# Inverse of cumulative decay products in a gated linear attention with a feed-forward layer: VectorE's reciprocal instead of ScalarE's logarithm and exponential with a Newton step

## The chip, the cores and the metric

The kernel runs on one core of one Trainium2 chip. The metric is the time of one execution on the device in microseconds (us); of several runs the median is given.

## What is computed

The reference is a gated linear recurrence for 4 batches of 8 heads, 768 tokens and a head dimension of 48, followed by a dense layer of two matrices on the 3072 tokens of width 384:

```
for t in range(S):
    state = alpha[:, :, t, :, None] * state + einsum('bhd,bhe->bhde', k[:, :, t], v[:, :, t])
    y[:, :, t] = einsum('bhd,bhde->bhe', q[:, :, t], state)
h  = x @ w_in                      # x is y, 3072 x 384; w_in is 384 x 2048
sp = maximum(h, 0) + log1p(exp(-abs(h)))
out = (h * erf(sp)) @ w_out        # w_out is 2048 x 384
```

All values of alpha lie between 0.8 and 1.

## The kernel before

**Chunks.** The recurrence is worked off in 24 chunks of 128 tokens, six for each batch, and all heads of a batch at once: a tile of 128 x 4 x 128 holds eight heads as four pairs, two heads above each other in the partitions, with the tokens along the free dimension. Inside a chunk, A is the running product of alpha. Queries are multiplied by A and keys by its inverse w, so that a masked product of the two gives all decays within the chunk; a state T carries what came before. The steps of a chunk are methods:

- ld loads alpha, k, q and v by SyncE's queue, and a ScalarE instruction (L141) notes values of alpha that are too large.
- a1 makes A by four scans of VectorE, one for each pair (L146; the trace calls the operation TENSOR_TENSOR_SCAN, the lists of instructions SCALAR_TENSOR_TENSOR), and GpSimd copies its last column (L151).
- a2 makes the inverse. ScalarE takes Ln of A (L155) into r, a tile in PSUM, and Exp of minus that (L156), which also sums r into flags. VectorE then makes a Newton step from r: A times r (L158), and (A r - 2) r (L159). The result w is minus the inverse.
- a3 makes K = k w (L164) and Q = q A (L166) on VectorE.
- a4 multiplies K and Q on TensorE for all pairs (pS, L174), masks the products on VectorE (sT, L180) with a mask of -1 and 0, which takes the minus sign out, and turns K for the state (pn, L187, and kn, L189).
- a5 multiplies with v and the state (py, L199 and L205), copies the result to y (L209), and brings the state T forward (L214, L224 for the first chunk of a batch, L228 and L229 for the others); the minus sign of K is undone there by a subtraction or by a factor of -1.
- a6 turns y into the block's x on TensorE (px, L254) and writes it as a high part (x_hi, ScalarE, L256) and a low part (x_lo, VectorE, L257).

**Blocks.** The dense layer works on 12 blocks of 256 tokens, two chunks each. H multiplies x by w_in (ph, L272, three matmuls for each pair of tiles for the high and low parts), and ScalarE reads it twice (w by Exp, L283, and hs, L284). L1 takes three functions of it on ScalarE (L289 to L291), L2 a Newton step on VectorE (t, L297, and w, L298). E switches ScalarE's table, applies Gelu (s, L303) and switches back. Z combines on VectorE (s, L308, and hs, L309). O splits the result into a high part gh (L320 on VectorE or L322 on ScalarE) and a low part gl (VectorE, L323), and multiplies both by w_out (acc, L331). The result goes out at L339.

**Weights.** They come as pairs of 32-bit words of a 64-bit number. Each of 28 pieces is put together by one ScalarE and three VectorE instructions (L360 to L368) and split into two parts (L343 on ScalarE, L344 on VectorE). All this lies in the first part of the run, among the steps of the first chunks.

**Order.** Three lists give the order of the steps: START (the weights, chunks 0 to 6 and the first blocks), ORDER (once for each block in between, with two chunks) and TAIL (the end). The framework's scheduler then lays out the instructions of each engine, and may put an instruction ahead of one that the lists give out earlier. Each engine works its own instructions in that order. Tiles of PSUM that the chunks use, r among them, come from one pool of four buffers (ps_at).

ScalarE's functions belong to tables. The helper tab ties the instructions that need the Ln and Exp table, L155 and L156 too, to the stretch between two table loads.

Of the kernel before, what the change touches and what calls it, by code (L numbers as in the profile page):

```python
# [10 lines left out]
F32 = mybir.dt.float32  # L11
# [4 lines left out]
AF = mybir.ActivationFunctionType  # L16
ALU = mybir.AluOpType
# [6 lines left out]
SAT = 4.0  # L24
RT2 = 2.0**0.5
LNEXP, GELU = "natural_log_exp_and_others", "gelu_and_others"
# The order in which the steps of chunks (128 tokens) and blocks (256) are given out: the start with the weights, the
# same for each block in between, and the end.
START, ORDER, TAIL = (
    z.split()  # L30
    for z in (
# [18 lines left out]
def gla_moe(ctx: ExitStack, tc: tile.TileContext, q, k, v, alpha, w_in, w_out, out):  # L50
    nc = tc.nc
    B, CPB, _, D, NP, P = q.shape
# [11 lines left out]
    const = ctx.enter_context(tc.tile_pool(name="const", bufs=1))  # L64
    fast = ctx.enter_context(ExitStack())
    raw = fast.enter_context(tc.tile_pool(name="raw", bufs=1))
    at = fast.enter_context(tc.tile_pool(name="at", bufs=2))
# [11 lines left out]
    for nm, fill in (("a", 1.0), ("q", 0.0), ("k", 0.0)):  # L79
# [3 lines left out]

    ident = const.tile([P, P], F32, name="ident")
    make_identity(nc, ident)
    maskn = const.tile([P, P], F32, name="maskn")
    nc.gpsimd.memset(maskn, -1.0)
    nc.gpsimd.affine_select(
        out=maskn, in_=maskn, pattern=[[1, P]], compare_op=ALU.is_ge, fill=0.0, base=0, channel_multiplier=-1
    )  # L90
    fixed = const.tile([P, 5], F32, name="fixed")
    floor, bhi, bsat, bone, ones = (fixed[:, n : n + 1] for n in range(5))
# [22 lines left out]
    def tab(ins):  # L115
        for p in phase["prev"]:
            tc.add_manual_dep(ins.ins, p.ins.name, NOSYNC, reason="tables")
        phase["cur"].append(ins)
        return ins
# [4 lines left out]
    class Chunk:  # L124
# [26 lines left out]
            nc.gpsimd.tensor_copy(out=self.ae, in_=self.A[:, :, P - 1])  # L151

        def a2(self):
            r = ps_at.tile([P, NP, P], F32, name="r", tag="at")
            tab(nc.scalar.activation(r, self.A, AF.Ln))  # L155
            tab(nc.scalar.activation(r, r, AF.Exp, scale=-1.0, accum_out=flags[:, self.n, 0:1]))  # L156
            w = at.tile([P, NP, P], F32, name="w", tag="w", bufs=1)
            nc.vector.tensor_tensor(out=w, in0=self.A, in1=r, op=ALU.mult)  # L158
            nc.vector.scalar_tensor_tensor(out=w, in0=w, scalar=2.0, in1=r, op0=ALU.subtract, op1=ALU.mult)  # L159
            self.w = w  # L160

        def a3(self):
# [5 lines left out]
        def a4(self):  # L168
            self.sT = []
            pss = [ps_at.tile([P, NP, P], F32, name="pS", tag="at") for _ in range(2)]  # L170
            for pair in range(NP):
                for par in range(2):
                    rows = slice(par * HD, par * HD + D)
                    nc.tensor.matmul(  # L174
                        out=pss[par][:, pair, :], lhsT=self.K[rows, pair, :], rhs=self.Q[rows, pair, :],
                        start=True, stop=True,
                    )
            for ps in pss:
                st = at.tile([P, NP, P], F32, name="sT", tag="sT")
                nc.vector.tensor_tensor(  # L180
                    out=st, in0=ps, in1=maskn.unsqueeze(1).broadcast_to([P, NP, P]), op=ALU.mult
                )
                self.sT.append(st)
            if not self.last:
                pn = ps_at.tile([P, NP, P], F32, name="pn", tag="at")
                for pair in range(NP):
                    nc.tensor.transpose(pn[:, pair, :], self.K[:, pair, :], ident)  # L187
                self.kn = at.tile([P, NP, 2, HD], F32, name="kn", tag="kn", bufs=1)
                nc.scalar.activation(  # L189
                    self.kn.rearrange("p a b d -> p (a b d)"), pn.rearrange("p a t -> p (a t)"), AF.Copy  # L190
                )

        def a5(self):
# [16 lines left out]
            if not self.last:  # L210
                pu = ps_at.tile([P, 512], F32, name="pu", tag="at")
                for pair in range(NP):
                    for par in range(2):
                        nc.tensor.matmul(  # L214
                            out=pu[par * HD : (par + 1) * HD, pair * D : (pair + 1) * D],
                            lhsT=self.kn[:, pair, par, :], rhs=vt[:, 2 * pair + par, :], start=True, stop=True,
                        )
                U = pu[:, : NP * D].rearrange("p (a d) -> p a d", a=NP)
                aeb = self.ae.unsqueeze(2).broadcast_to([P, NP, D])
                for par in range(2):  # L220
                    rows = slice(par * HD, (par + 1) * HD)
                    Tp, Up, ap = T[rows, :, par, :], U[rows], aeb[rows]
                    if self.first:
                        nc.vector.scalar_tensor_tensor(  # L224
                            out=Tp, in0=Up, scalar=-1.0, in1=ap, op0=ALU.mult, op1=ALU.mult
                        )
                    else:
                        nc.vector.tensor_tensor(out=Tp, in0=Tp, in1=Up, op=ALU.subtract)  # L228
                        nc.vector.tensor_tensor(out=Tp, in0=Tp, in1=ap, op=ALU.mult)  # L229

        def a6(self, moe):
# [6 lines left out]
    class Moe:  # L238
# [7 lines left out]
            self.x = (x_hi, x_lo)  # L246

        def turn(self, y, c, pool, tag):
            """Writes the 128 tokens of y, transposed, to the block's x as two parts."""
            x_hi, x_lo = self.x  # L250
            cs = slice(c * P, (c + 1) * P)
            px = pool.tile([P, 512], F32, name="px", tag=tag)
            for kt in range(KT):
                nc.tensor.transpose(px[:, kt * P : (kt + 1) * P], y[:, kt * P : (kt + 1) * P], ident)  # L254
            pxv = px[:, : KT * P].rearrange("p (a t) -> p a t", a=KT)
            nc.scalar.activation(x_hi[:, :, cs], pxv, AF.Copy)  # L256
            nc.vector.tensor_tensor(out=x_lo[:, :, cs], in0=pxv, in1=x_hi[:, :, cs].bitcast(F32), op=ALU.subtract)  # L257
# [86 lines left out]
        nc.vector.tensor_tensor(out=lo, in0=src, in1=hi.bitcast(F32), op=ALU.subtract)  # L344

    def weight(hi, lo, src, n, pool, tag):
        """Loads a matrix of float32, or of float64 as pairs of int32, and splits it into two parts."""
        if src.dtype == F32:
            t = pool.tile([P, n], F32, name="wst", tag=tag)
            nc.sync.dma_start(out=t, in_=src)  # L350
# [1 line left out]
            return  # L352
        st = pool.tile([P, n, 2], I32, name="wst", tag=tag)
        nc.sync.dma_start(out=st.rearrange("p n two -> p (n two)"), in_=src.bitcast(I32))
        # The scale takes 112 from the exponent that a high word has as a float32: its 5 low bits are left, and
        # what float32 has no exponent for goes to zero. Shifted by 3, the word ends where a float32's would.
        low, high = st[:, :, 0], st[:, :, 1].bitcast(F32)
        buf = keep_w.tile([P, 1024], F32, name="wbuf", tag="w")
        y, z = buf[:, :n], buf[:, 512 : 512 + n].bitcast(I32)
# [19 lines left out]
        weight(wo_hi[:, f, :], wo_lo[:, f, :], w_out[f * P : (f + 1) * P, :], DM, keep_s, "s")  # L379

    def general():
        """Any inputs: the recurrence token by token, then the same layers."""
        with ExitStack() as es:
            dram = es.enter_context(tc.tile_pool(name="g_dram", bufs=1, space=bass.MemoryType.DRAM))
            NG4 = P // (B * H)
# [69 lines left out]
    moes = [Moe(i * TB, pools) for i in range(NBLK)]  # L455

    def run(order, c0, b0):
        """The steps of a list: a chunk's count from c0, a block's (after @) from b0; past the end there are none."""
        for step in order:
            name, _, rel = step.partition("@")  # L460
            name, *arg = name.split("_")
# [20 lines left out]
        run(ORDER, 2 * i + 3, i)  # L482
    run(TAIL, 2 * NBLK, NBLK - 1)

    # lanes with a sum of inverse products, a gain, or an exponential past what the way above can carry
    top = const.tile([P, 3], F32, name="top")
    nc.vector.tensor_reduce(
        out=top[:, 0:2], in_=flags.rearrange("p n two -> p two n"), op=ALU.max, axis=mybir.AxisListType.X
# [54 lines left out]
```

## Time and profile before

| | us |
|---|---|
| median of 2 runs | 597.95 |
| the 2 runs | 597.25 and 598.65 |
| span of the profiled execution, first to last instruction | 594.3 |
| busy, PE (TensorE) | 552.4 |
| busy, DVE (VectorE) | 503.0 |
| busy, ACT (ScalarE) | 485.1 |

The profiled execution has a span and no time of its own on the page; the runs' median stands 3.65 us above that span. In rows of the profile a group is a line of the kernel, an engine, an operation and its tiles, with the count, then the busy time in us and the mean of one in ns, and then the engine's idle time just before them with what ended it. Rows in order of time begin with the start in us and the duration in us. Matmuls overlap, so their durations add up to more than PE's busy time.

### The profile page before, as it was taken

The page shows a single profiled execution, that of the slowest core. Times are in us where ns is not written, and L with a number is a line of the kernel's source. Part 1 is how long each engine was busy: PE and PEld are TensorE (multiplying, and loading weights), DVE is VectorE, ACT ScalarE, POOL GpSimd, SP SyncE. Part 2 cuts the span into 40 slices and gives each one's busy share as a digit, 9 for nine tenths or more (in the row PEclk, how much of TensorE's full clock was granted, in tenths as well). Part 3 has the DMA queues.
Part 4 walks back from the last instruction along what each step waited for, and adds up shares of the span by engine and source line. Part 5 has one row for each costly group of instructions (what it writes and reads, how often), then busy time and mean ns, then how long its engine had stood idle before and what let it go on. Part 6 is the DMA issues. An engine that isn't in the chain of part 4 may idle for free.

```text
span 594.3 us, 11033 instructions
## 1 busy us (share of the span) xinstructions
PE 552.4 (93%) x4282; PEld 534.8 (90%) x4282; DVE 503.0 (85%) x769; ACT 485.1 (82%) x845; POOL 20.9 (4%) x40
## 2 busy tenths in 40 slices
PE   0679798999999999999999999999999999999994
PEld 0568787999999999999999999999999999999884
DVE  7899999999999869869779879879779879758780
ACT  4558979698989879889879879889788888889941
POOL 1000110002000000000000000000000000000000
PEclk9999798998999999999999999999999999999998
DMA  6584312313112102112112102112112101000001
GB/s 196 176 290 145 110 55 81 120 54 94 28 41 81 41 26 68 41 29 68 40 28 68 41 28 67 41 39 70 28 35 66 34 28 41 1 1 28 1 27 33
DMA packets 20220, 36.98 MB, mean 62 GB/s; under 512 B 3520, under 2 KB 9664, under 8 KB 20160
## 3 DMA queue, kind: packets, MB, share of 16 engines
q1 hardware_dynamic: 20160, 36.19, 19.9%
q8 instruction: 36, 0.59, 0.4%
q14 instruction: 24, 0.20, 0.1%
HBM read 31.46 MB, written 4.72 MB: 61 GB/s over the span
## 4 chain that ended last, share of the span: by engine, by line
PE 81%; DVE 9%; ACT 6%; DMA 2%; issue 1%; SPq 0%; ACTq 0%; DVEq 0%
PE acc L331 33%; PE ph L272 30%; PE py L205 7%; PE pS L174 4%; PE py L199 3%; PE pu L214 2%; DMA wst<-in_moe_w_in_dram 2%; PE pn L187 1%; PE px L254 1%; DVE hs L309 1%; DVE s L308 1%; DVE A L146 1%; ACT wbuf L360 1%; ACT w L283 1%; DVE wbuf L365 1%
## 5 line engine op out<-in xcount | busy, mean ns | idle before, releaser
L272 PE MATMUL ph<-x_hi,wi_hi 128*128 128x256 f32 x576 | 164.0, 288 | 4.0 <-ACT hs L284 3.4
L272 PE MATMUL ph<-x_lo,wi_hi 128*128 128x256 f32 x576 | 163.4, 284 | 0.4 <-DVE x_lo L257 0.4
L272 PE MATMUL ph<-x_hi,wi_lo 128*128 128x256 f32 x576 | 163.2, 284 | 0.0
L331 PE MATMUL acc<-wo_hi,gh 128*128 128x384 f32 x384 | 134.5, 351 | 3.6 <-DVE gh L320 2.6
L331 PE MATMUL acc<-wo_lo,gh 128*128 128x384 f32 x384 | 131.3, 342 | 0.0
L331 PE MATMUL acc<-wo_hi,gl 128*128 128x384 f32 x384 | 130.0, 344 | 1.2 <-DVE gl L323 1.2
L272 PEld LDWEIGHTS ph<-x_hi,wi_hi 128*128 128x128 f32 x576 | 110.4, 192 | 5.8 <-ACT hs L284 4.2
L272 PEld LDWEIGHTS ph<-x_lo,wi_hi 128*128 128x128 f32 x576 | 110.5, 192 | 0.7 <-DVE x_lo L257 0.7
L272 PEld LDWEIGHTS ph<-x_hi,wi_lo 128*128 128x128 f32 x576 | 110.5, 192 | 0.5 <-DVE wi_lo L344 0.5
L283 ACT ACTIVATE w<-ph 128x512 f32<-128x512 f32 x96 | 57.5, 599 | 46.9 <-PE ph L272 44.0
L297 DVE TENSOR_TENSOR t<-s,w 128x1024 f32<-128x1024 f32 x48 | 58.5, 1219 | 29.4 <-ACT w L291 29.3
L331 PEld LDWEIGHTS acc<-wo_hi,gh 128*128 128x128 f32 x384 | 72.8, 190 | 5.3 <-DVE gh L320 2.6
L331 PEld LDWEIGHTS acc<-wo_hi,gl 128*128 128x128 f32 x384 | 72.2, 190 | 2.6 <-DVE gl L323 2.6
L323 DVE TENSOR_TENSOR gl<-hs,gh 128x512 fp32r<-128x512 f32 x96 | 65.3, 683 | 10.8 <-ACT gh L322 10.3
L331 PEld LDWEIGHTS acc<-wo_lo,gh 128*128 128x128 f32 x384 | 73.2, 191 | 0.0
L205 PE MATMUL py<-raw_v,sT 128*128 128x48 f32 x384 | 57.9, 279 | 5.5 <-DVE sT L180 5.5
L308 DVE TENSOR_TENSOR s<-s,w 128x1024 f32<-128x1024 f32 x48 | 58.2, 1218 | 2.3 <-ACT s L303 2.1
L205 PEld LDWEIGHTS py<-raw_v,sT 128*128 128x128 f32 x384 | 53.8, 203 | 6.8 <-DVE sT L180 6.6
L298 DVE SCALAR_TENSOR_TENSOR w<-t,w 128x1024 f32<-128x1024 f32 x48 | 58.4, 1217 | 0.4
L309 DVE SCALAR_TENSOR_TENSOR hs<-s,hs 128x1024 f32<-128x1024 f32 x48 | 58.2, 1217 | 0.3
L289 ACT ACTIVATE s<-w,fixed 128x1024 f32<-128x1024 f32 x48 | 55.1, 1151 | 0.0
L284 ACT ACTIVATE hs<-ph 128x512 f32<-128x512 f32 x96 | 54.8, 593 | 0.0
(67 smaller groups left out, 834.2 us busy)
## 6 DMA issues: line engine op xcount, KB each, us to landing
wst<-in_moe_w_in_dram SPq DMA_DIRECT2D x12, 512.0 KB, 4.6
wst<-in_moe_w_out_dram SPq DMA_DIRECT2D x16, 384.0 KB, 3.4
raw_a<-in_alpha_dram SPq DMA_DIRECT2D x48, 96.0 KB, 2.2
raw_k<-in_k_dram SPq DMA_DIRECT2D x48, 96.0 KB, 2.2
raw_q<-in_q_dram SPq DMA_DIRECT2D x48, 96.0 KB, 2.2
raw_v<-in_v_dram SPq DMA_DIRECT2D x24, 192.0 KB, 2.4
out_dram<-o SPq DMA_DIRECT2D x24, 192.0 KB, 1.9
```

The source lines that it names most:

```text
L174: nc.tensor.matmul(out=pss[par][:, pair, :], lhsT=self.K[rows, pair, :], rhs=self.Q[rows, pair, :], start=True, stop=True,)
L205: nc.tensor.matmul(out=py[:, h * D : (h + 1) * D], lhsT=self.sT[par][:, pair, :], rhs=vt[:, h, :], start=self.first, stop=self.first or pa ...
L272: nc.tensor.matmul(out=o, lhsT=wt[:, kt, fs], rhs=xt[:, kt, :], start=n == 0, stop=n == 3 * KT - 1)
L283: tab(nc.scalar.activation(w, ph, AF.Exp, accum_out=self.pl.flags[:, n : n + 1]))
L284: nc.scalar.activation(self.hs[g][:, sl], ph, AF.Copy)
L289: tab(nc.scalar.activation(s, w, AF.Ln, bias=bone))
L297: nc.vector.tensor_tensor(out=t, in0=s, in1=w, op=ALU.mult)
L298: nc.vector.scalar_tensor_tensor(out=w, in0=t, scalar=2.0, in1=w, op0=ALU.subtract, op1=ALU.mult)
L308: nc.vector.tensor_tensor(out=s, in0=s, in1=w, op=ALU.mult)
L309: nc.vector.scalar_tensor_tensor(out=h, in0=s, scalar=RT2 / 2, in1=h, op0=ALU.add, op1=ALU.mult)
L323: nc.vector.tensor_tensor(out=gl.rearrange("p a t -> p (a t)"), in0=gg, in1=ghf.bitcast(F32), op=ALU.subtract)
L331: nc.tensor.matmul(out=self.acc[tt][:, :DM], lhsT=gt[:, u, ts], rhs=wt[:, f, :], start=f == 0 and n == 0, stop=f == NF - 1 and n == 2,)
```

## The change

The step a2 becomes one reciprocal on VectorE, of A straight into w. ScalarE's Ln and Exp go. A Copy on ScalarE, whose only use is its sum into flags, takes the place of the sum that Exp gave; it reads w and writes a tile of the pool ps_at that nothing reads, and it isn't tied to a table. As w is now the inverse itself and not minus it, the mask is +1 and 0, the state is added to instead of subtracted from, and in the first chunk of a batch a plain product takes the place of the one with a factor of -1. The rest of the diff blanks comments. In the changed kernel, lines after a2 stand two lines higher, and lines after the update of the state in a5 four.

```diff
-    maskn = const.tile([P, P], F32, name="maskn")
-    nc.gpsimd.memset(maskn, -1.0)
+    mask = const.tile([P, P], F32, name="mask")
+    nc.gpsimd.memset(mask, 1.0)
...
         def a2(self):
-            r = ps_at.tile([P, NP, P], F32, name="r", tag="at")
-            tab(nc.scalar.activation(r, self.A, AF.Ln))
-            tab(nc.scalar.activation(r, r, AF.Exp, scale=-1.0, accum_out=flags[:, self.n, 0:1]))
             w = at.tile([P, NP, P], F32, name="w", tag="w", bufs=1)
-            nc.vector.tensor_tensor(out=w, in0=self.A, in1=r, op=ALU.mult)
-            nc.vector.scalar_tensor_tensor(out=w, in0=w, scalar=2.0, in1=r, op0=ALU.subtract, op1=ALU.mult)
+            nc.vector.reciprocal(w, self.A)
+            junk = ps_at.tile([P, NP, P], F32, name="sum", tag="at")
+            nc.scalar.activation(junk, w, AF.Copy, accum_out=flags[:, self.n, 0:1])
             self.w = w
...
                     if self.first:
-                        nc.vector.scalar_tensor_tensor(
-                            out=Tp, in0=Up, scalar=-1.0, in1=ap, op0=ALU.mult, op1=ALU.mult
-                        )
+                        nc.vector.tensor_tensor(out=Tp, in0=Up, in1=ap, op=ALU.mult)
                     else:
-                        nc.vector.tensor_tensor(out=Tp, in0=Tp, in1=Up, op=ALU.subtract)
+                        nc.vector.tensor_tensor(out=Tp, in0=Tp, in1=Up, op=ALU.add)
                         nc.vector.tensor_tensor(out=Tp, in0=Tp, in1=ap, op=ALU.mult)
```

The scheduler lays out the engines' instructions anew. Three places show how. All three are in the block whose sT of the first chunk starts at 246.85 us in the trace of before. Numbers behind a name count the tiles in the order in which the program makes them.

The first place is VectorE at the first chunk of this block (chunk 12). Before, the four scans of A, the sT of the chunk ahead, and then Q and the block's Newton steps t and w:

```order
L323 TENSOR_TENSOR gl_2909<-hs_2177,gh_2908 128x512
L146 SCALAR_TENSOR_TENSOR A_2963<-raw_a_91,fixed_105 128x128 x3
L180 TENSOR_TENSOR sT_2730<-pS_2720,maskn_102 128x512
L180 TENSOR_TENSOR sT_2732<-pS_2721,maskn_102 128x512
L166 TENSOR_TENSOR Q_2978<-raw_q_93,A_2963 128x512
L297 TENSOR_TENSOR t_2905<-s_2821,w_2654 128x1024
L298 SCALAR_TENSOR_TENSOR w_2654<-t_2905,w_2654 128x1024
L297 TENSOR_TENSOR t_2960<-s_2956,w_2698 128x1024
L323 TENSOR_TENSOR gl_2925<-hs_2177,gh_2924 128x512
```

And now:

```order
L319 TENSOR_TENSOR gl_2885<-hs_2157,gh_2884 128x512
L146 SCALAR_TENSOR_TENSOR A_2939<-raw_a_91,fixed_105 128x128 x4
L155 RECIPROCAL w_2946<-A_2939 128x512
L178 TENSOR_TENSOR sT_2706<-pS_2696,mask_102 128x512
L178 TENSOR_TENSOR sT_2708<-pS_2697,mask_102 128x512
L293 TENSOR_TENSOR t_2881<-s_2797,w_2630 128x1024
L162 TENSOR_TENSOR K_2950<-raw_k_95,w_2946 128x512
L294 SCALAR_TENSOR_TENSOR w_2630<-t_2881,w_2630 128x1024
L164 TENSOR_TENSOR Q_2952<-raw_q_93,A_2939 128x512
L146 SCALAR_TENSOR_TENSOR A_3086<-raw_a_91,fixed_105 128x128 x4
L293 TENSOR_TENSOR t_2936<-s_2932,w_2674 128x1024
L319 TENSOR_TENSOR gl_2901<-hs_2157,gh_2900 128x512
```

The reciprocal follows the scans at once and stands ahead of the two sT; K and the next chunk's scans have moved ahead of the second t and of the gl behind it.

The second place is VectorE further on in the same block, from x_lo of the chunk ahead. Before:

```order
L257 TENSOR_TENSOR x_lo_2553<-px_2852,x_hi_2552 128x3x128
L323 TENSOR_TENSOR gl_2941<-hs_2242,gh_2940 128x512
L158 TENSOR_TENSOR w_2973<-A_2963,r_2970 128x512
L159 SCALAR_TENSOR_TENSOR w_2973<-w_2973,r_2970 128x512
L146 SCALAR_TENSOR_TENSOR A_3112<-raw_a_91,fixed_105 128x128
L164 TENSOR_TENSOR K_2976<-raw_k_95,w_2973 128x512
L297 TENSOR_TENSOR t_3021<-s_3017,w_2756 128x1024
L146 SCALAR_TENSOR_TENSOR A_3112<-raw_a_91,fixed_105 128x128
L298 SCALAR_TENSOR_TENSOR w_2756<-t_3021,w_2756 128x1024
L146 SCALAR_TENSOR_TENSOR A_3112<-raw_a_91,fixed_105 128x128 x2
L166 TENSOR_TENSOR Q_3145<-raw_q_93,A_3112 128x512
L323 TENSOR_TENSOR gl_3002<-hs_2242,gh_3001 128x512
```

And now:

```order
L253 TENSOR_TENSOR x_lo_2531<-px_2828,x_hi_2530 128x3x128
L319 TENSOR_TENSOR gl_2917<-hs_2222,gh_2916 128x512
L155 RECIPROCAL w_3093<-A_3086 128x512
L293 TENSOR_TENSOR t_2995<-s_2991,w_2732 128x1024
L162 TENSOR_TENSOR K_3115<-raw_k_95,w_3093 128x512
L319 TENSOR_TENSOR gl_2976<-hs_2222,gh_2975 128x512
L294 SCALAR_TENSOR_TENSOR w_2732<-t_2995,w_2732 128x1024
L304 TENSOR_TENSOR s_2793<-s_2793,w_2339 128x1024
L178 TENSOR_TENSOR sT_2964<-pS_2954,mask_102 128x512
L178 TENSOR_TENSOR sT_2966<-pS_2955,mask_102 128x512
L305 SCALAR_TENSOR_TENSOR hs_2338<-s_2793,hs_2338 128x1024
L304 TENSOR_TENSOR s_2797<-s_2797,w_2630 128x1024
```

Here the reciprocal is the second chunk's (chunk 13): where the first chunk's pair L158 and L159 stood, it stands now, a chunk earlier in the order; before, the second chunk's pair came only behind the next x_lo.

The third place is ScalarE at the same x_hi and x_lo. Before:

```order
L256 ACTIVATE x_hi_2552<-px_2852 128x3x128
L155 ACTIVATE r_2970<-A_2963 128x512
L322 ACTIVATE gh_2940<-hs_2242 128x512
L156 ACTIVATE r_2970,flags_111<-r_2970 128x512
L290 ACTIVATE w_2756<-s_3017 128x1024
L291 ACTIVATE w_2756<-w_2756 128x1024
```

And now:

```order
L252 ACTIVATE x_hi_2530<-px_2828 128x3x128
L157 ACTIVATE sum_2948,flags_111<-w_2946 128x512
L318 ACTIVATE gh_2916<-hs_2222 128x512
L286 ACTIVATE w_2732<-s_2991 128x1024
L141 ACTIVATE junk_3036,flags_111<-raw_a_91,fixed_105 128x512
L287 ACTIVATE w_2732<-w_2732 128x1024
```

The Copy for the sum stands where Ln stood, and behind it gh, the block's second Ln and the note on alpha, which has moved ahead of the block's Exp.

More of the change, by code (lines that the diff above doesn't have):

```diff
@@ L85, in gla_moe @@
     make_identity(nc, ident)
-    maskn = const.tile([P, P], F32, name="maskn")
-    nc.gpsimd.memset(maskn, -1.0)
+    mask = const.tile([P, P], F32, name="mask")
+    nc.gpsimd.memset(mask, 1.0)
     nc.gpsimd.affine_select(
-        out=maskn, in_=maskn, pattern=[[1, P]], compare_op=ALU.is_ge, fill=0.0, base=0, channel_multiplier=-1
+        out=mask, in_=mask, pattern=[[1, P]], compare_op=ALU.is_ge, fill=0.0, base=0, channel_multiplier=-1
     )
@@ L180, in a4 @@
                 nc.vector.tensor_tensor(
-                    out=st, in0=ps, in1=maskn.unsqueeze(1).broadcast_to([P, NP, P]), op=ALU.mult
+                    out=st, in0=ps, in1=mask.unsqueeze(1).broadcast_to([P, NP, P]), op=ALU.mult
                 )
```

## The prediction

> **What bounds the kernel now.** I read the busy shares and the forty slices of the page first, then the busy times by stage, then the groups of VectorE and ScalarE, and last the instructions of one block in order of time.
>
> ```profile
> span 594.3 us, 11033 instructions
> PE 552.4 (93%) x4282; PEld 534.8 (90%) x4282; DVE 503.0 (85%) x769; ACT 485.1 (82%) x845; POOL 20.9 (4%) x40
> PE   0679798999999999999999999999999999999994
> DVE  7899999999999869869779879879779879758780
> ACT  4558979698989879889879879889788888889941
> PEclk9999798998999999999999999999999999999998
> ```
>
> No engine has much room. TensorE (PE) leads over the whole, but VectorE (DVE) is full in slices 2 to 13, and there PE is not yet. So the span has to be cut into stages. Here are the stages, with the busy time of each engine in them:
>
> ```profile
> core 0: us, PE busy (x) PEld busy (x) DVE busy (x) ACT busy (x) POOL busy (x), PEclk, DMA share, GB/s
> 0.00:42.00 42.00, 19.18 (x119) 17.06 (x120) 35.05 (x72) 22.40 (x44) 3.92 (x19) 1.00 0.67 217
> 42.00:130.00 88.00, 79.51 (x614) 74.78 (x615) 87.14 (x157) 75.62 (x144) 4.98 (x3) 0.94 0.34 103
> 130.00:196.10 66.10, 65.54 (x516) 63.96 (x515) 62.48 (x95) 59.43 (x103) 5.17 (x4) 0.97 0.20 58
> 240.20:372.50 132.30, 132.30 (x1072) 129.58 (x1072) 112.04 (x163) 114.06 (x197) 3.02 (x6) 1.00 0.15 46
> 372.50:504.90 132.40, 132.40 (x1073) 129.69 (x1072) 112.14 (x164) 113.35 (x195) 3.02 (x6) 1.00 0.14 42
> 504.90:594.30 89.40, 79.40 (x539) 76.56 (x538) 56.77 (x68) 62.05 (x98) 0.00 (x0) 0.97 0.04 15
> ```
>
> From 42 to 130 us VectorE works 87.14 of 88 us while it splits the weights: it bounds this stage, and any microsecond more on it is a microsecond more of time. From 130 us PE works 65.54 of 66.10. In the steady blocks PE works every microsecond: 132.3 us for three blocks, so 44.1 us a block, with VectorE at 112.04, so 37.35 us a block, and 6.75 us of idle. After 504.9 us there are no chunks left.
>
> **The change part by part.** These groups carry the prices (busy us, then mean ns of one):
>
> ```profile
> L146 DVE TENSOR_TENSOR_SCAN A<-raw_a,fixed 128x128 f32<-128x128 f32 x96 | 35.1, 406 | 0.0
> L158 DVE TENSOR_TENSOR w<-A,r 128x512 f32<-128x512 f32 x24 | 16.4, 684 | 8.7 <-ACT r L156 8.6
> L159 DVE SCALAR_TENSOR_TENSOR w<-w,r 128x512 f32<-128x512 f32 x24 | 16.4, 682 | 0.3
> L344 DVE TENSOR_TENSOR wo_lo<-wbuf,wo_hi 128x384 fp32r<-128x384 f32 x16 | 8.7, 546 | 0.0
> L155 ACT ACTIVATE r<-A 128x512 f32<-128x512 f32 x24 | 14.4, 599 | 1.9 <-DVE A L146 1.9
> L156 ACT ACTIVATE r<-r 128x512 f32<-128x512 f32 x24 | 14.3, 594 | 0.1
> L229 DVE TENSOR_TENSOR T<-T,ae 64x192 f32<-64x192 f32 x32 | 11.3, 353 | 0.8
> L224 DVE SCALAR_TENSOR_TENSOR T<-pu,ae 64x192 f32<-64x192 f32 x8 | 2.8, 352 | 0.3 <-PE pu L214 0.2
> ```
>
> *Removed from VectorE*, per chunk: L158 and L159, 0.684 + 0.682 = 1.366 us. *Removed from ScalarE*: Ln and Exp, 0.599 + 0.594 = 1.193 us. *Added to ScalarE*: one Copy of the same shape with the accumulator, which I price as L155, 0.6 us; the accumulator's read stays. ScalarE so gets about 0.6 us a chunk lighter. VectorE also no longer waits for r, 8.6 us in all.
>
> *Added to VectorE*: one reciprocal of 128x512. No row shows a division, so it has to be bounded. From below: one pass. Tensor operations of 384 and 512 elements take 0.546 and 0.684 us, so an element costs (0.684 - 0.546) / 128 = 1.08 ns and the instruction 0.13 us beside; a one-pass reciprocal is 0.68 us. The scan, where each element needs the one before, takes 0.406 us for 128, which is (0.406 - 0.13) / 128 = 2.2 ns an element: so VectorE does have instructions that need more than one pass, and at that rate the reciprocal takes 1.2 us. From above: a quotient found bit by bit has 24 of them, 24 passes of 0.55 us, 13.4 us. Between ends so far apart I take what a full-precision reciprocal costs in VectorE's own steps: each Newton step (L158 and L159, 1.366 us) doubles the good bits, and three of them take 3 or 4 bits to 24. 3 x 1.366 = **4.1 us**. Long division is serial in its nature like the scan, which is why I lean to several passes and not to one.
>
> [...]
>
> So each chunk adds 4.1 - 1.37 = 2.73 us to VectorE.
>
> *The start, 7 chunks (0 to 6).* 7 x 2.73 = 19.1 us on the engine that bounds it. Against that: the waits for r there, 1.8 us, go, and of the 66.10 - 62.48 = 3.6 us idle between 130 and 196 us a part, say 1.5 us, is filled.
>
> ```profile
> DVE w L158 <- ACT r L156: 1.8, 3, 0.8
> ```
>
> That leaves **+16 us**. In the first 42 us the shifted chunks do not decide, since PE is busy 19.18 us only and what follows is VectorE's queue anyway; but that queue is one engine, and nothing else of it moves away.
>
> *The steady blocks, 17 chunks in 8.5 blocks.* By sums VectorE goes to 37.35 + 2 x 2.73 = 42.8 of 44.1 us: still under PE. What counts is where the reciprocals stand. This is one block of before, first VectorE, then PE (start us, us):
>
> ```profile
> 246.85 1.26 DVE L180 TENSOR_TENSOR sT<-pS,maskn 128x512 f32<-128x512 f32 x2
> 253.70 1.23 DVE L297 TENSOR_TENSOR t<-s,w 128x1024 f32<-128x1024 f32 x1 [2.58 <-ACT w L291]
> 254.84 0.68 DVE L323 TENSOR_TENSOR gl<-hs,gh 128x512 fp32r<-128x512 f32 x1
> 259.72 0.56 DVE L257 TENSOR_TENSOR x_lo<-px,x_hi 128x384 fp32r<-128x384 f32 x1 [3.06 <-ACT x_hi L256]
> 270.78 1.28 DVE L180 TENSOR_TENSOR sT<-pS,maskn 128x512 f32<-128x512 f32 x2
> 271.98 0.42 DVE L320 CAST gh<-hs 128x512 fp32r<-128x512 f32 x1
> ```
>
> ```profile
> 255.16 0.57 PE L205 MATMUL py<-raw_v,sT 128*128 128x48 f32 x4
> 258.00 0.34 PE L331 MATMUL acc<-wo_hi,gl 128*128 128x384 f32 x1
> 260.53 0.28 PE L272 MATMUL ph<-x_lo,wi_hi 128*128 128x256 f32 x1
> 274.83 0.44 PE L331 MATMUL acc<-wo_hi,gh 128*128 128x384 f32 x1
> ```
>
> The first reciprocal of the block now stands just ahead of the two sT at 246.85. They would end at 252.2 instead of 248.1, and PE reads them at 255.16: covered. Behind it the new order has t, K, w, Q, the next chunk's four scans, t, gl, w, Q, x_lo. Added up from 246.85 with a step of 1.14 us for the wide ones, 0.6 for the narrow and 0.34 for a scan, gl ends near 258.7 and x_lo near 261.0; PE wants them at 258.00 and 260.53. The two idle spells of 2.58 and 3.06 us have hidden most, and 0.5 to 0.7 us is left as PE's wait. The second reciprocal stands behind x_lo and the gl after it. By the same walk the sT stay near 270.5 and gh comes at 273.9 instead of 271.98, against 274.83: just covered, with the gl behind it a few tenths late. What hides each piece are these idle spells; without them a block would pay 2 x 2.73 = 5.5 us. So a block's loss lies between 0 and 5.5 us. With 1.3 us of VectorE idle left in 44.1 there is no room for the many small waits of an engine that runs in order; I take 0.7 us for the gl and x_lo, and as much again for the rest: 1.4 x 8.5 = **+12 us**.
>
> *The added wait on ScalarE.* The Copy waits for the reciprocal, and behind it stand gh, the block's next Ln and, for the second chunk, x_hi. By the walk the reciprocals end near 250.9 and 265.8 us, and the Copies come up behind the x_hi near 259 and the gh near 275: nothing waits. If VectorE ran a further 8 us late, this wait would pass its lateness on to PE.
>
> *The signs* (mask of +1, add for subtract, a tensor product in place of L224) exchange operations of one price, 0.352 against 0.353 us: nothing.
>
> *Sum.* 594.3 + 16 + 12 = 622.3 us of span. The page gives no time around the span; the median of the runs shown, 597.95, is 3.65 above it, and I add that: **626 us**.
>
> **The rivals.**
>
> 1. *One pass; not slower.* The reciprocal costs what any tensor operation of 512 elements does, 0.68 us, and VectorE loses 0.68 us a chunk. It decides below 1.37 us, the price of the pair it replaces, and so holds at the scan's 1.2 us too. Only the start gains: 7 x 0.68 = 4.8 us and a wait for r of 1.8, less what PE does not let through after 130 us, where it works 65.54 of 66.10: some 4 us. The steady blocks are PE's at 100% and give nothing. 594 us. For it: every row of VectorE but the scan is at one pass. Against: no such row divides.
>
> 2. *All hidden in the steady blocks.* At 4 us or somewhat less, the new order lays the reciprocals into the 6.75 us of idle, and only the start pays: 597.95 + 16 = 614 us. For it: both idle spells of the block lie behind the first reciprocal. Against: the 0.5 to 0.7 us above.
>
> 3. *VectorE becomes the bound everywhere.* From a reciprocal of 1.37 + 6.75 / 2 = 4.7 us on, a block takes as long as VectorE does. At 8 us: 37.35 + 2 x 6.63 = 50.6 us, 6.5 us more in 8.5 blocks, 55 us, and 7 x 6.63 - 3.3 = 43 us in the start: 696 us.
>
> That the change would not do what it says I leave out: the sum of w is the sum that the Exp gave, so the same lanes are flagged.
>
> **How the numbers follow.** The forecast has 0.52, its own range 612 to 650, from 0.5 to 3 us a block and a price of 3.3 to 4.5 us; the first rival 0.25, the second 0.13, the third 0.10. The range of 593 to 655 takes in the first rival's middle and leaves out the third. A measurement of this kernel can tell about 2%, so 586.0 to 609.9 us is no change. Slower is the forecast and two rivals: 0.75. Within 2% is nearly all of the first rival, 0.23. Faster 0.02.
>
> **What would show it.** The group of the reciprocal gives its mean: near 4.1 us for the forecast, 0.7 or 1.2 for the first rival, over 4.7 for the third. The steady blocks' period should be 45 to 46 us with VectorE over 42 us in it, and PE should wait for gl, x_lo or sT in them, where it now waits for nothing. The stretch in which PE works every microsecond should begin some 16 us later. I am wrong in the mechanism if the reciprocal is long and yet the start does not grow, or if PE's waits name ScalarE instead; wrong in size if a block loses 3 us or more.

## The result and the profile after

The changed kernel takes 626.31 us (median of 2 runs, 626.22 to 626.40) against 597.95 us before: a ratio of 1.0496 [1.045, 1.0541], slower. The page of its profiled execution has these totals and slices:

```profile
span 624.4 us, 11013 instructions
PE 562.4 (90%) x4282; PEld 540.1 (86%) x4282; DVE 549.2 (88%) x745; ACT 474.9 (76%) x821; POOL 11.7 (2%) x40
PE   0368759999799999999999999999999999999994
DVE  7989996999999999998998998998989989749681
ACT  3447963968878877978888788789789779679941
PEclk9997866998889999999999999999999999999998
```

VectorE is busy 549.2 us instead of 503.0. PE's unbroken row of nines begins four slices later than before, and PEclk has a seven, an eight and two sixes in slices 4 to 7, where before it had a nine, a seven, a nine and an eight.

The cost is in the groups of VectorE (busy us, mean ns of one, idle time ahead and what ended it):

```profile
L155 DVE RECIPROCAL w<-A 128x512 f32<-128x512 f32 x24 | 80.4, 3351 | 8.5 <-ACT junk L141 7.9
```

One reciprocal takes 3.35 us; the pair of Newton instructions that it replaces took 1.366. So a chunk adds 1.985 us to VectorE, and 24 of them 47.6 us, of which the span shows 30.

**Where the 30 us lie.** ScalarE copies y once a chunk, on the path from attention to the rest, so its start dates a chunk. Here are chunk 9, the last one before the two traces settle into steady blocks, and chunk 23, the last of all, first of before and then of after (start us, us):

```profile
213.37 0.49 ACT L209 ACTIVATE y<-py 128x384 f32<-128x384 f32 x1 [0.95 <-PE py L205]
522.47 0.49 ACT L209 ACTIVATE y<-py 128x384 f32<-128x384 f32 x1 [0.95 <-PE py L205]
```

```profile
241.78 0.49 ACT L207 ACTIVATE y<-py 128x384 f32<-128x384 f32 x1 [0.49 <-PE py L203]
552.30 0.49 ACT L207 ACTIVATE y<-py 128x384 f32<-128x384 f32 x1 [0.95 <-PE py L203]
```

At chunk 9 the changed kernel is 241.78 - 213.37 = 28.4 us late, at chunk 23 it is 29.8 us late. The fourteen chunks between, seven blocks, lose 1.4 us together: the period goes from 44.16 to 44.36 us. Practically the whole loss is made in the start, and there by chunk 7, whose y starts at 196.33 us instead of 168.61: 27.7 us late. Of the 1.4 us, 1.1 are busy time of PE (310.19 instead of 309.10 us between these two rows), and no row names a cause for them.

Two of the five stages into which the first 225.30 us of after were cut, and the sum of all five:

```profile
core 0: us, PE busy (x) PEld busy (x) DVE busy (x) ACT busy (x) POOL busy (x), PEclk, DMA share, GB/s
42.00:130.00 88.00, 69.61 (x495) 63.97 (x496) 80.28 (x129) 60.99 (x116) 2.96 (x3) 0.79 0.29 88
130.00:172.00 42.00, 36.20 (x253) 33.45 (x251) 39.87 (x60) 33.12 (x59) 0.38 (x2) 0.90 0.25 73
sum 225.30, PE 173.90 PEld 161.86 DVE 205.62 ACT 155.06 POOL 6.75; mean PE 34.78 PEld 32.37 DVE 41.12 ACT 31.01 POOL 1.35
```

The same sum of before, over its first 196.1 us, in which PE gets through nearly the same work (1245 matmuls, 1252 in after):

```profile
sum 196.10, PE 164.23 PEld 155.80 DVE 184.68 ACT 157.45 POOL 14.06; mean PE 41.06 PEld 38.95 DVE 46.17 ACT 39.36 POOL 3.51
```

The start is 29.2 us longer. On VectorE it splits into 205.62 - 184.68 = 20.9 us of more work, which is ten reciprocals at 1.985 us and a microsecond of other rows, and 19.7 - 11.4 = 8.3 us of more idle time. VectorE is the fullest engine there in both kernels, and yet it waits more than before. These are waits of three engines in the first 225 us of after, of VectorE the two for pu (us in total, times, longest):

```profile
ACT sum L157 <- DVE w L155: 13.9, 5, 3.7
PE px L250 <- ACT y L207: 8.6, 2, 8.0
PE py L203 <- ACT wbuf L356: 7.5, 1, 7.5
PE py L203 <- DVE sT L178: 4.7, 4, 2.8
DVE T L224 <- PE pu L212: 4.7, 3, 3.6
DVE T L222 <- PE pu L212: 3.6, 1, 3.6
```

VectorE waits 8.3 us for pu here and waited 0.6 us for it before; this is nearly all of its additional idle time. Before, PE never waited more than 0.6 us for y. The row that names wbuf is to be read with care: py reads raw_v and sT and not wbuf, and it starts at 28.29 us, with the sT of 27.50 us just ahead of it, so it more likely waited for that. The longest of these waits, 8.0 us, reads as a chain in the timeline of after:

```profile
41.79 3.35 DVE L155 RECIPROCAL w<-A 128x512 f32<-128x512 f32 x1
45.17 0.60 ACT L157 ACTIVATE sum<-w 128x512 f32<-128x512 f32 x1 [2.15 <-DVE w L155]
45.59 1.15 DVE L361 SCALAR_TENSOR_TENSOR wbuf<-wbuf 128x512 int32<-128x512 int32 x2
46.66 1.15 DVE L364 SCALAR_TENSOR_TENSOR wbuf<-wbuf 128x512 int32<-128x512 int32 x2
47.38 0.63 ACT L339 ACTIVATE wi_hi<-wbuf 128x512 fp32r<-128x512 f32 x1 [1.49 <-DVE wbuf L364]
48.33 0.47 ACT L207 ACTIVATE y<-py 128x384 f32<-128x384 f32 x1
48.85 0.90 PE L250 MATMUL px<-ident,y 128*128 128x128 f32 x3 [8.00 <-ACT y L207]
```

The reciprocal holds VectorE from 41.79 to 45.1 us. ScalarE stands at the Copy meanwhile, then at wi_hi, whose wbuf VectorE works on only behind the reciprocal, and y stands behind both in ScalarE's order. PE, which wants y, has nothing from 40.85 to 48.85 us. ScalarE's two waits for VectorE in it are 2.15 + 1.49 = 3.6 us; the rest is mostly work of its own that its order puts ahead of y.

**The steady blocks.** Of the waits of PE from 240 to 540 us one row is left:

```profile
PE ph L268 <- DVE x_lo L253: 0.3, 1, 0.3
```

Two stages of nearly three blocks each (three take 132.8 us), in the same view by stage, give PE all the time and VectorE 122.89 and 122.42 us of it, so about 41 us a block instead of 37.35:

```profile
269.50:402.00 132.50, 132.48 (x1069) 129.33 (x1068) 122.89 (x157) 110.82 (x191) 2.04 (x6) 1.00 0.16 46
402.00:534.00 132.00, 132.00 (x1068) 128.93 (x1067) 122.42 (x156) 110.21 (x189) 2.04 (x6) 1.00 0.14 42
```

This is VectorE in the block that the prediction walked through (its sT then at 246.85, now at 277.98), and below it PE's first matmuls that need the gl and the x_lo of it:

```profile
274.71 3.35 DVE L155 RECIPROCAL w<-A 128x512 f32<-128x512 f32 x1
277.98 1.22 DVE L178 TENSOR_TENSOR sT<-pS,mask 128x512 f32<-128x512 f32 x2
285.17 0.68 DVE L319 TENSOR_TENSOR gl<-hs,gh 128x512 fp32r<-128x512 f32 x1
288.80 0.56 DVE L253 TENSOR_TENSOR x_lo<-px,x_hi 128x384 fp32r<-128x384 f32 x1 [1.21 <-ACT x_hi L252]
291.58 3.35 DVE L155 RECIPROCAL w<-A 128x512 f32<-128x512 f32 x1 [0.95 <-ACT junk L141]
```

```profile
286.88 0.34 PE L327 MATMUL acc<-wo_hi,gl 128*128 128x384 f32 x1
289.62 0.28 PE L268 MATMUL ph<-x_lo,wi_hi 128*128 128x256 f32 x1
```

gl ends at 285.85 us, 1.0 us before PE reads it, and x_lo at 289.36, 0.3 us before. VectorE even idles 1.21 us ahead of x_lo. Both reciprocals of the block lie wholly beside PE's work. VectorE's wait for r, which was to go, has a successor: the reciprocals have 8.5 us of idle time ahead of them in all, none of it among the waits of the first 225 us; as PE waits for 0.3 us in all in these blocks, that costs nothing.

### The profile page after: what moved, and what is told of

It is laid out like the page before. It is cut to its first block, busy times and chain, and to the rows that moved or that the text cites. A ratio compares the mean times of both kernels' runs of the same rounds, so it can differ in the third digit from the quotient of the medians.

```text
span 624.4 us, 11013 instructions
## 1 busy us (share of the span) xinstructions
PE 562.4 (90%) x4282; PEld 540.1 (86%) x4282; DVE 549.2 (88%) x745; ACT 474.9 (76%) x821; POOL 11.7 (2%) x40
## 4 chain that ended last, share of the span: by engine, by line
PE 66%; DVE 5%; ACT 2%; issue 1%; DMA 0%; DVEq 0%; ACTq 0%
PE acc L327 27%; PE ph L268 25%; PE py L203 5%; PE pS L172 3%; PE py L197 2%; PE pu L212 1%; PE pn L185 1%; PE px L250 1%; DVE w L155 1%; DVE s L304 1%; DVE hs L305 1%; DVE A L146 1%; DVE gl L319 0%; DVE w L294 0%; DMA out_dram<-o 0%
## 5 line engine op out<-in xcount | busy, mean ns | idle before, releaser
L268 PE MATMUL ph<-x_hi,wi_hi 128*128 128x256 f32 x576 | 165.9, 291 | 5.6 <-ACT hs L280 3.2
L327 PE MATMUL acc<-wo_hi,gl 128*128 128x384 f32 x384 | 131.4, 347 | 1.4 <-DVE gl L319 1.3
L155 DVE RECIPROCAL w<-A 128x512 f32<-128x512 f32 x24 | 80.4, 3351 | 8.5 <-ACT junk L141 7.9
```

The costliest lines, as they stand in the source:

```text
L155: nc.vector.reciprocal(w, self.A)
L268: nc.tensor.matmul(out=o, lhsT=wt[:, kt, fs], rhs=xt[:, kt, :], start=n == 0, stop=n == 3 * KT - 1)
L327: nc.tensor.matmul(out=self.acc[tt][:, :DM], lhsT=gt[:, u, ts], rhs=wt[:, f, :], start=f == 0 and n == 0, stop=f == NF - 1 and n == 2,)
```

## The experiments

The first theory after the result was that the 1.985 us a chunk are paid where VectorE is the bound, in the start, and hidden in the steady blocks. Its rivals were that the signs, the steady blocks, ScalarE's Copy, or the order that the scheduler lays out anew cost the time. Each expectation names the theories that it weighs. All ratios are to the kernel before, timed beside each experiment on the same chip; its own runs lay between 593.8 and 600.5 us there.

The table gives for each profile how late y of chunk 9 and of chunk 23 start, by their rows, against 213.37 and 522.47 us of before, and what the seven blocks between lose (differences are taken before rounding):

| kernel | chunk 9 late, us | chunk 23 late, us | lost between, us |
|---|---|---|---|
| the changed kernel | 28.4 | 29.8 | 1.4 |
| e1_signs | 2.7 | 2.7 | 0.0 |
| e2_late | 2.7 | 3.9 | 1.3 |
| e3_early | 28.0 | 28.1 | 0.0 |
| e4_short | 6.5 | 8.0 | 1.5 |
| e5_nosum | 24.8 | 28.0 | 3.1 |
| e6_short_nosum | 9.7 | 14.2 | 4.5 |
| e7_nonewton | -0.1 | 2.2 | 2.3 |
| e8_split | 24.2 | 25.7 | 1.5 |
| e9_short_aorder | 16.1 | 17.3 | 1.2 |
| e10_recip_sorder | 35.5 | 55.8 | 20.2 |
| e11_recip_border | 23.2 | 38.0 | 14.8 |
| e12_nonewton_border | -2.0 | -2.0 | 0.0 |

e1_signs has the instructions in the order of before and is no slower than it by the medians, so up to some 3 us of such a lag is the difference between two executions.

**e1_signs: the signs alone.**

```diff
-            nc.vector.tensor_tensor(out=w, in0=self.A, in1=r, op=ALU.mult)
-            nc.vector.scalar_tensor_tensor(out=w, in0=w, scalar=2.0, in1=r, op0=ALU.subtract, op1=ALU.mult)
+            nc.vector.scalar_tensor_tensor(out=w, in0=self.A, scalar=-1.0, in1=r, op0=ALU.mult, op1=ALU.mult)
+            nc.vector.scalar_tensor_tensor(out=w, in0=w, scalar=2.0, in1=r, op0=ALU.add, op1=ALU.mult)
```

This is the changed kernel with Ln, Exp and the Newton step kept; the lines show its Newton step against that of before, and the mask and the state have the changed signs.

> The change without its reciprocal: Ln, Exp and a Newton step as before, with the new signs (mask of +1, state added). Theory A (the length of the reciprocal on VectorE, in the start): as before, 596 to 600 us. Rival C (the new order and the new signs cost something themselves): above 605 us.

Measured: 596.17 us against 596.97, 0.9993 [0.9966, 1.0021]. The signs cost nothing.

**e2_late and e3_early: the reciprocal only in the steady chunks, and only in the early ones.**

```diff
+            if self.n >= 10:      # e3_early: if self.n < 10
                 w = at.tile([P, NP, P], F32, name="w", tag="w", bufs=1)
                 nc.vector.reciprocal(w, self.A)
...
+            else:
+                r = ps_at.tile([P, NP, P], F32, name="r", tag="at")
+                tab(nc.scalar.activation(r, self.A, AF.Ln))
...
```

> Reciprocal and Copy only in the 14 chunks from number 10 on; chunks 0 to 9 keep Ln, Exp and Newton. Theory A (only the stage before the steady blocks pays, the steady blocks hide theirs): 597 to 601 us. Rival B (every chunk pays alike, 28.4 / 24 = 1.18 us): 598 + 14 x 1.18 = 614.5 us.

> Reciprocal and Copy only in the 10 chunks 0 to 9; the later ones keep Ln, Exp and Newton. Theory A: the whole loss, 624 to 628 us. Rival B: 598 + 10 x 1.18 = 610 us.

Measured: e2_late 598.06 us, 1.0015 [0.9992, 1.0038]; e3_early 624.66 us, 1.0458 [1.0424, 1.0492]. Both lie where theory A had them. The fourteen late reciprocals cost nothing that can be measured, and the ten early ones cost all of it. That the steady blocks pay is refuted. The stage of e3_early that answers to the first one above is nearly the same row:

```profile
42.00:130.00 88.00, 69.77 (x497) 64.11 (x498) 80.33 (x130) 60.83 (x116) 2.97 (x3) 0.79 0.29 87
```

**e4_short: one pass in place of the reciprocal.**

```diff
-            nc.vector.reciprocal(w, self.A)
+            nc.vector.tensor_tensor(out=w, in0=self.A, in1=self.A, op=ALU.mult)
```

> The changed kernel with a plain product A x A (one pass, about 0.68 us) in place of the reciprocal, so that w isn't the inverse and the rest of the recurrence computes with it. Theory A (the instruction's length): 592 to 597 us, a little below before, since VectorE loses one instruction a chunk in the stage that it bounds. Rival C (the wiring: the Copy that waits in ScalarE's queue, the new order): above 605 us.

The row of the stand-in shows what it asks of VectorE:

```profile
L155 DVE TENSOR_TENSOR w<-A 128x512 f32<-128x512 f32 x24 | 16.5, 689 | 10.0 <-ACT junk L141 9.7
```

Measured: 604.09 us, 1.0108 [1.0076, 1.014]. Two things follow. With a short instruction most of the loss is gone, so the length counts. But VectorE works only 491.9 us here, 11 us less than before, ScalarE is lighter too, and the kernel is still some 1% slower: something beside the length costs time, and it costs it in the start (6.5 us late at chunk 9). The expectations had no such case. The difference is under the 2% that count as faster or slower here, but its interval is clear of 1.

**e5_nosum and e6_short_nosum: without ScalarE's Copy.** Both leave out the sum of w, so the flags on w are not set; e6 has the product of e4 as well.

```diff
-            junk = ps_at.tile([P, NP, P], F32, name="sum", tag="at")
-            nc.scalar.activation(junk, w, AF.Copy, accum_out=flags[:, self.n, 0:1])
```

> The changed kernel without the Copy on ScalarE: the sum of the inverse isn't taken, its flag stays 0. Theory A (the length of the reciprocal alone): 624 to 627 us, as the changed kernel. Rival D (the Copy, which waits for the reciprocal at the head of ScalarE's queue, 13.9 us in the start, holds up what stands behind it): 614 to 619 us.

> As the short stand-in A x A, and without the Copy, so that a chunk has neither the reciprocal nor its sum and w isn't the inverse. Rival D: the 7 us that the stand-in stood above before go, 592 to 597 us. Rival C' (the new order of the start, with VectorE no longer the bound): they stay, 601 to 605 us.

Measured: e5_nosum 622.68 us, 1.041 [1.0348, 1.0473], which can't be told from the changed kernel's 1.0496 [1.045, 1.0541]; e6_short_nosum 609.23 us, 1.0196 [1.0147, 1.0244]. Both lie outside the ranges of their two theories. Rival D had 614 to 619 us for e5, so a loss of the size of the 13.9 us that ScalarE stands at the Copy in the start isn't there; but e5 has an order of its own, so its 3.6 us are no clean price of the Copy. e6 does strictly less work than e4 and is slower by 5 us. No engine has more to do for it, but the scheduler lays out the order anew for every program. So a third theory was formed, that the order by itself costs time; e9 to e12 test it.

**e7_nonewton: no VectorE step at all.** Ln and Exp write w directly; the Newton step is left out, so w has only the accuracy of ScalarE's functions.

```diff
-            nc.vector.reciprocal(w, self.A)
-            junk = ps_at.tile([P, NP, P], F32, name="sum", tag="at")
-            nc.scalar.activation(junk, w, AF.Copy, accum_out=flags[:, self.n, 0:1])
+            tab(nc.scalar.activation(w, self.A, AF.Ln))
+            tab(nc.scalar.activation(w, w, AF.Exp, scale=-1.0, accum_out=flags[:, self.n, 0:1]))
```

> Ln and Exp on ScalarE write the inverse straight to w, and VectorE's Newton step is left out, so that the inverse has only the accuracy of ScalarE's functions. VectorE loses 1.37 us in each chunk, 13.7 us in the ten of the start. Theory A (VectorE bounds the start): 584 to 592 us. Rival E (VectorE is no bound there once it is relieved a little; PE and ScalarE are): 594 to 600 us.

Measured: 597.4 us, 1.0004 [0.9976, 1.0031]: VectorE's work falls from 503.0 to 478.3 us, and nothing is gained, as rival E had it. Read alone, this says that VectorE's length doesn't decide. But its order is a new one as well, so it is inconclusive without e12.

**e8_split: four short reciprocals instead of one long.**

```diff
-            nc.vector.reciprocal(w, self.A)
+            for pair in range(NP):
+                nc.vector.reciprocal(w[:, pair, :], self.A[:, pair, :])
```

> The changed kernel with four reciprocals of 128x128 in place of one of 128x512. If an element costs 6.25 ns and an instruction 0.15 us, one of them takes 0.95 us and the four overlap to some 3.5 us: 625 to 630 us, same as the changed kernel. If most of the 3.35 us is a fixed cost of the instruction, four of them take over 8 us and the time goes past 680 us.

Measured: 622.42 us, 1.0425 [1.0372, 1.0478], a little under the first range, and not to be told from the changed kernel. Cut in four, with room for other instructions between the pieces, it costs the same as far as this can tell. The two kernels also give the price by size (ns, least/median/most), of e8_split and of after:

```profile
L156 DVE RECIPROCAL w<-A x96: 883/896/954, 12.0 to 513.2; 128x128 f32<-128x128 f32 x96
```

```profile
L155 DVE RECIPROCAL w<-A x24: 3343/3353/3355, 12.2 to 512.1; 128x512 f32<-128x512 f32 x24
```

(3353 - 896) / 384 = 6.4 ns an element, and 896 - 128 x 6.4 = some 77 ns beside. What the prediction calls one pass, the tensor operations of 384 and 512 elements that take 0.546 and 0.684 us in before, was at 1.08 ns an element.

**e9_short_aorder and e10_recip_sorder: the two instructions in each other's order.** Every engine's instructions are tied together in a stored order, so that the scheduler has no choice:

```diff
+        for one, two in zip(line, line[1:]):
+            tc.add_manual_dep(here[two], one, NOSYNC, reason="order")
```

e9 has the one-pass product of e4 in the order of the changed kernel, e10 the reciprocal in the order of e4.

> The stand-in A x A (0.68 us, w isn't the inverse) with every engine held to the changed kernel's order, so that against the changed kernel only the instruction's length differs, 2.66 us a chunk. Theory A (length, paid in the ten chunks of the start): 599 to 604 us. Rival C (the changed kernel's order costs most of the loss): 612 to 620 us.

> The reciprocal with every engine held to the order that the scheduler chose for the stand-in. Theory A: the stand-in's 604 us and 22 to 27 us of length, 626 to 631 us. Rival C: an order that was not laid out for the long instruction loses more, over 635 us.

Measured: e9 611.4 us, 1.023 [1.0189, 1.027]; e10 653.12 us, 1.0934 [1.0878, 1.0991]. Length alone, in whatever order, would have left e9 near e4 and e10 near the changed kernel; both are well above that, e10 by 27 us. Rival C's ranges came nearest: e10 lies in its range and e9 just under it. With the changed kernel and e4 this fills a square:

| | one pass, 0.69 us | reciprocal, 3.35 us | difference |
|---|---|---|---|
| order laid out for one pass | 604.1 | 653.1 | 49.0 |
| order laid out for the reciprocal | 611.4 | 626.3 | 14.9 |

The difference of the instructions is 24 x 2.66 = 64 us of VectorE. The order made for the short one lets 49 us of it through, the order made for the long one 15. That order in turn is 7 us worse for the short instruction.

The start says the same. e9 is 16.1 us late at chunk 9, though its VectorE has less to do than before; only the other 12.3 of the changed kernel's 28.4 us come and go with the length while the order is held. And VectorE's waits for pu are there with the short instruction too, so they aren't made by the length. This is e9 in the same stretch of the run:

```profile
DVE T L386 <- PE pu L374: 6.1, 3, 3.6
DVE T L384 <- PE pu L374: 4.9, 2, 3.9
```

The waits of PE in e10 from 250 to 560 us show part of why its steady blocks now lose 20 us, which the changed kernel's don't:

```profile
PE acc L488 <- DVE gl L480: 8.6, 5, 1.8
PE py L364 <- DVE sT L339: 2.3, 4, 1.0
```

They are the waits that the prediction had expected of the change: gl and sT late by 1 to 2 us, in an order that was laid out with a short instruction in the reciprocal's place. They make up 10.9 of the 20 us. Another 8.7 are busy time of PE: between the y of chunks 9 and 23 it works 317.82 us on the matmuls that took it 309.10 before, at a mean granted clock of 0.98 instead of 1.00.

**e11_recip_border and e12_nonewton_border: in the order of before.** e11 has the reciprocal without the Copy (the flags on w are not set), e12 is e7 (no Newton step), both tied to the kernel before's order as in e9.

> The reciprocal without the Copy for its sum (its flag stays 0), with every engine held to the order of the kernel before; the reciprocal stands where the first instruction of the Newton pair stood. Against the kernel before VectorE has 1.99 us more a chunk and ScalarE 1.4 us less. Theory A (only length, ten chunks): 612 to 619 us. Rival C (the scheduler's new order was no worse than the old one): 621 to 626 us, as the changed kernel without the Copy, which took 622.7.

> Ln and Exp straight to w without the Newton step, with every engine held to the order of the kernel before; the inverse has only ScalarE's accuracy. VectorE loses 1.37 us a chunk and nothing is moved. Theory A (VectorE bounds the start): 585 to 592 us. Rival E (it bounds it only upwards; with less on it PE and ScalarE bound): 594 to 598 us.

Measured: e11 633.49 us, 1.0612 [1.0563, 1.0661], above what any theory expected; e12 591.25 us, 0.9903 [0.9868, 0.9937]. PE's waits in e11 from 240 to 540 us:

```profile
PE acc L485 <- DVE gl L477: 6.6, 6, 1.4
PE py L361 <- DVE sT L336: 2.1, 4, 0.9
```

In the order of before the steady blocks lose 14.8 us; with the order laid out for it, the same program (e5) loses 3.1. In the start it is 23.2 against 24.8: the new order saves there nothing. VectorE waits for pu only 0.6 us in the start of e11, as before. And e12 settles e7, since the two differ in the order alone: with the order held, taking VectorE's pair away does gain, about 1%; in e7 a new order gave that back. That is some 6 us for 13.7 us less of VectorE's work in the first ten chunks, so not every microsecond of it there is a microsecond of time. e12 is faster than both kernels, but only by leaving out the Newton step, so it is no replacement where w has to be as accurate as before.

## Why the prediction was right, and where it was wrong

The time was forecast at 626 us and is 626.31. That is closer than its working was: two terms were off by 10 to 12 us each, in opposite directions, and that they cancel to 0.3 us is luck.

*The price of the reciprocal.* Forecast 4.1 us as three Newton steps, measured 3.35: that an element costs several times what it does in a one-pass operation, 6.4 against 1.08 ns, is right, and the size is 0.75 us too high. Whether these are passes no run shows. 3.35 us are 2.45 Newton steps of 1.366 us; the picture of three of them was the author's estimate, and nothing in the runs supports it.

*The start, forecast +16 us.* Measured 28.4 us at chunk 9, and 27.7 already at chunk 7: this step failed in size. Eight chunks make nearly all of it and not seven, but at the measured price eight are 8 x 1.985 = 15.9 us, so neither the count nor the price made it short. What failed is the sum itself, VectorE's added work less the idle time that it fills. The 3.3 us that were taken off weren't there; VectorE's idle time grew by 8.3 us, nearly all of it in waits for pu. These come with the new order: they are in e9 (11.0 us), which has that order and a short instruction, and not in e11 (0.6 us), which has the reciprocal, without the Copy, in the order of before. With the order of the changed kernel held, the length makes 12.3 of the 28.4 us; in the order of before it makes 23.2. So the loss doesn't divide into a share of length and a share of order that hold by themselves. What the Copy and the clock have in it was not separated.

*The steady blocks, forecast +12 us.* Measured 1.4 us: this step failed, in part through the price. The walk had gl end near 258.7 us against 258.00 and x_lo near 261.0 against 260.53. With 3.35 instead of 4.1 us both come 0.75 us sooner, near 257.95 and 260.25, and are hidden. In the trace gl has more room than that, 1.0 us, and x_lo 0.3 us. The "as much again for the rest" had no row behind it, and no row shows it. VectorE's 41 us of 44.36 leave some 3.3 us of room where the forecast had 1.3. e2_late shows the same by itself.

*The Copy on ScalarE, "nothing waits".* Right in the steady blocks, where ScalarE shows no wait for w. Wrong in the start, where it stands 13.9 us at it; the walk was made for a steady block only. What this is worth stays open: e5, without the Copy and in an order of its own, was 3.6 us faster, and that is within the noise.

*The signs.* Nothing, as forecast; shown by e1.

*What lies around the span.* 3.65 us were added; 626.31 - 624.4 = 1.9 us are there. So the span was forecast at 622.3 and is 624.4. The 3.65 us set a profiled execution against the median of two others; in every run whose own span is on record it is under 2 us.

*The rivals.* The one pass is refuted by the price, and its 594 us would have been wrong even at one pass: e4 takes 604. The second rival had the mechanism of the steady blocks right, at "4 us or somewhat less", and took the same 16 us for the start; with 28 it would have come to 626. The third needed 4.7 us. By mechanism it was the second that came true, by time the forecast.

*What would show it.* The period stayed at 44.36 us (45 to 46 forecast), VectorE at about 41 us (over 42), PE's steady waits at 0.3 us, and PE's last wait of more than 0.3 us ahead of the steady blocks ends 30 us later (172.42 instead of 142.66 us) instead of 16. One of the signs of a wrong mechanism came up in the start: behind the wait for the first chunk's Q (17.7 us; before, 15.8 for its K) the longest of PE's there names ScalarE, 8.6 us for y, against 4.7 us for VectorE's sT. The chain above leads part of that back to VectorE, and the rest to the place of y in ScalarE's order, which the prediction didn't look at.

*What no step had.* That the scheduler's order is part of the price. The prediction walked through the new order at one place, in a steady block, and costed the instruction; but the same reciprocal costs 15 us over a one-pass instruction in one order and 49 in another, and in the start the new order is 16.1 us late even with a one-pass instruction.

## What to carry to other kernels

Cut the span at the point from which the bounding engine works without a break, and price a longer instruction in the chunks ahead of it without taking idle time off: in the order of before, the start paid 23.2 us for 19.9 us of added work in ten chunks. In the blocks behind that point compare each consumer's start with the producer's end: in after x_lo ended 0.3 us before PE read it, and the seven blocks lost 1.4 us; in e11 gl came up to 1.4 us late and sT up to 0.9, PE waited 8.7 us for them, and the blocks lost 14.8. Where a scheduler lays out the order, the new order is a term of its own, as large here as the length. So look at its start too, and not only at a steady block, and hold the order fixed before an experiment with an instruction of another length is read.

## What the runs showed of the hardware

VectorE's reciprocal of fp32 took 3.35 us for 512 elements of a partition (after) and 0.90 us for 128 (e8_split), which is 6.4 ns an element between the two sizes; the tensor operations of 384 and 512 elements took 0.546 and 0.684 us (before), which is 1.08 ns an element, a sixth of that.

In after the granted clock was down for longer than the waits of PE around it lasted: two waits of 5.48 us together, and 17.06 us at a clock of 0.50. In the timeline a reciprocal is followed by the two waits, and the matmuls of 256 columns are back at 0.28 us only 12.8 us behind the second wait:

```profile
84.89 3.35 DVE L155 RECIPROCAL w<-A 128x512 f32<-128x512 f32 x1
89.05 0.74 PE L197 MATMUL py<-T,Q 128*128 128x96 f32 x2 [2.70 <-ACT sum L157]
92.57 1.26 PE L203 MATMUL py<-raw_v,sT 128*128 128x48 f32 x4 [2.78 <-DVE sT L178]
105.00 0.41 PE L268 MATMUL ph<-x_lo,wi_hi 128*128 128x256 f32 x1
105.38 0.28 PE L268 MATMUL ph<-x_hi,wi_hi 128*128 128x256 f32 x1
```

The granted clock (the third number from the end) in stretches there, and last in one of an earlier spell:

```profile
84.83:88.24 3.41, 1.52 (x20) 1.16 (x18) 3.41 (x3) 0.86 (x3) 0.19 (x1) 1.00 0.20 58
88.24:91.65 3.41, 0.74 (x2) 0.50 (x2) 3.41 (x5) 2.37 (x5) 0.00 (x0) 0.50 0.37 106
95.07:98.48 3.41, 3.41 (x29) 3.32 (x28) 0.11 (x1) 0.77 (x2) 0.00 (x0) 0.50 0.00 0
101.89:105.30 3.41, 3.41 (x18) 3.19 (x16) 3.41 (x7) 0.00 (x0) 1.03 (x1) 0.50 0.12 34
50.69:54.10 3.41, 3.41 (x16) 3.16 (x16) 3.41 (x8) 1.52 (x3) 0.00 (x0) 0.50 0.23 93
```

PE works 1.52 of the 3.41 us up to 88.24 us at a granted clock of 1.00. Then the clock is at 0.50, and it stays there to 105.30 us, though PE is busy throughout from 92.57 us: 12.7 us at 0.50, in which a matmul of 256 columns takes 0.41 instead of 0.28 us. In the trace's record of the clock, each spell at 0.50 in the first 225 us of after is a multiple of 3.41 us long, and together they are 51.2 us; in the first 196.1 us of before they are 13.65 us.

The two spells shown end differently. The one that ends at 54.10 us ends with one stretch of 3.41 us that PE filled with matmuls of 256 columns, and from 54.10 to 57.51 us the clock is at 1.00. In the other the stretches from 95.07 to 101.89 us are as full, 3.41 of 3.41 us each, mostly with matmuls of 48 to 128 columns, and the clock stays at 0.50 up to 105.30 us. What makes the difference was not tried, nor what brings the clock down.

Over the start PE's busy time for nearly the same work rose from 164.23 to 173.90 us, so by these two sums slower matmuls and what hangs on them account for an estimated 9.7 us of PE's time at most; how much of this is on the path was not tried.
